# A gated MLP in two passes over its width, its factors fetched one by one, its instructions in a fixed order

## The chip, the cores and the metric

The kernel runs on one core of a Trainium2 chip. Its time is device microseconds of one execution; the median of three runs of the kernel before is 918.9 us (915.48 to 921.77).

## The reference

Attention, a first MLP and a second, gated MLP follow one another on 2304 tokens of width 512; the second MLP is what the change rewrites.

```python
x = attention(q, k, v, M_prev, z_prev, beta)          # 4 x 576 tokens, 8 heads of 64
h = x @ w_in                                          # 512 -> 1024
e = exp(h - max(h)); solu = h * e / sum(e)
x = layernorm(solu) * g_ln @ w_out                    # 1024 -> 512
gate = 1 / (1 + exp(-(x @ w_gate)))                   # 512 -> 1536
out = (gate * (x @ w_val)) @ w_out2                   # 1536 -> 512
```

The weights of both MLPs arrive as 64-bit floats; the chip has none, so the kernel builds 32-bit values out of their integer halves.

## The kernel before, in words

**Precision.** Products run in a reduced 32-bit format. Each operand is split into a high part (a cast, on ACT) and a low part (value minus high part, on DVE or GpSimd), and a product is three matmuls: high x high, high x low, low x high.

**Attention** (to about 200 us) and the **first MLP** (to about 451 us) come first. The first MLP goes through 18 blocks of 128 tokens: hidden products (line 634), statistics on DVE, ACT and GpSimd, transposes (681), the output product (691, copied out at 697). Its steps are a list; the conversions of the first six width blocks of the second MLP (`EARLY = 6`) are merged evenly into it from step 60 on.

**The second MLP** cuts its width 1536 into 12 blocks of 128 (`f`) and the tokens into three groups of 768 (`s`), each in halves of 384. One unit is one (`s`, `f`). Value and gate of a unit are 2 x 2 block products over (halves of tokens, halves of width 512), done with seven products instead of eight: `left` names the weight sides v1, g0, g1, s1 to s4, sums of the blocks, and b11, t1, ... the token sides. Each product is six matmuls of 384 columns (893) into one of two PSUM buffers. ACT copies the first out (910), DVE's additions the others (912, 914, 916, 919, 920, 931, 938), ACT applies the sigmoid (936), GpSimd multiplies gate and value (942), `hilo` splits the result G (138 on ACT, 139 on DVE). `project` (951) multiplies G by the output factor into six PSUM banks, one for 128 tokens, which gather all 12 units of a group; these 18 matmuls are slipped between the products of the next unit by `fill`. So 36 units stand in three segments of 12.

**Conversion** of a block `f` (`convert`, `stage`): three raw loads (104: value, gate, output), for each two DVE operations (108, 109), two on ACT (112, 792), two on DVE (117, 122) and a multiplication on GpSimd (794); four GpSimd sums (808 to 811); a cast of all seven sides on ACT (815) and one GpSimd subtraction over 1792 columns for their low parts (816); the same for the output block (821, 822). The result stands in a ring of buffers (`ring_g`, `ring_o`) and is stored to DRAM (832), from where later segments fetch it (837), seven sides in one DMA of 1792 KB. Blocks 6 to 11 are converted in the first segment, while its units run; `prep` hands out their steps at each `fill`.

**Between segments** `xsplit` builds the next group's token sides: differences on GpSimd (859), casts on ACT (852), low parts on DVE (853).

**Order.** All DMAs are issued by SP's queue. Attention's instructions stand in a written order (`manual_schedule`); those of both MLPs are ordered by the framework's planner by its own costs. Each engine takes its instructions strictly in the order of its queue.

Of the kernel before, what the change touches and what calls it, by code (L numbers as in the profile page):

```python
# [32 lines left out]
def f32(ap):  # L33
    return ap.bitcast(F32)
# [13 lines left out]
def kernel(  # L48
# [16 lines left out]
    nc = tc.nc  # L65
# [36 lines left out]
    def load_raw(raw, src):  # L102
        a = src.shape[1]
        nc.sync.dma_start(raw.rearrange("p (a n) t -> p a (n t)", a=a), src)
# [478 lines left out]
    class Moe1:  # L583
# [33 lines left out]
        def hidden(self, t):  # L617
# [21 lines left out]
            def stats():  # L639
# [13 lines left out]
                sq = sb.tile([P, F1], BF16, tag="sq", name=f"sq{t}", bufs=1)  # L653
# [10 lines left out]
        def lntrans(self, t):  # L664
# [3 lines left out]
            def half(h):  # L668
                if t % GB == 0 and h == 0:

                    if g == 2:
                        L = [self.spare.tile([P, NF1, GW], F32R, tag="gv", name=f"lnT{g}{x}", bufs=2) for x in range(2)]
# [74 lines left out]
    EARLY = 6  # L747

    class Moe2:

        def __init__(self, ra, w3, xe, scr):
            self.ra, self.w3, self.xe, self.scr = ra, w3, xe, scr
            self.n, self.rb = [0, 0], None
            self.W, self.x, self.G = {}, None, {}
            self.tt, self.ttag = xe, "xs"
            self.dram = {}

        def ring_g(self, f):
            k = self.n[0]
            self.n[0] += 1  # L760
            pool = self.ra if self.rb is None else (self.ra, self.ra, self.rb)[k % 3]
            t = pool.tile([P, 2, 7, 2 * P], F32R, tag="gv", name=f"gv{f}_{k}", bufs=2 if pool is self.ra else 1)
            self.W.setdefault(f, [None, None])[0] = t
            return t

        def ring_o(self, f):
            k = self.n[1]
            self.n[1] += 1
            pool = self.ra if self.rb is None else (self.ra, self.w3, self.w3)[k % 3]
            t = pool.tile([P, 2, DM], F32R, tag="w3", name=f"wo2{f}_{k}", bufs=1 if pool is self.ra else 2)  # L770
            self.W.setdefault(f, [None, None])[1] = t
            return t

        def scratch(self, f):
            if f not in self.dram:
                self.dram[f] = [
                    self.scr.tile([P, 2, w], F32, tag=f"{x}{f}", name=f"scr{x}{f}") for x, w in (("g", 14 * P), ("o", DM))
                ]
            return self.dram[f]

        def convert(self, f, cv):

            st = {}

            def stage(src, dst):
                raw = cv.tile([P, 512, 2], I32, tag="raw", name="raw2", bufs=2)
                ex = cv.tile([P, 2, 512], I32, tag="ex", name="ex2", bufs=2)
                e, m = ex[:, 0], ex[:, 1]
                load_raw(raw, src)
                f64_a(raw, e, m)  # L790
                f64_r(e)
                nc.scalar.mul(f32(m), m, 2.0**-20)  # L792
                f64_b(raw, e, m, 2.0**-20)
                nc.gpsimd.tensor_mul(f32(m) if dst is None else dst, f32(m), f32(e))  # L794
                return f32(m)

            def val():
                st["gv"] = self.ring_g(f)
                st["M"] = cv.tile([P, 8, 2 * P], F32, tag="M", name=f"M{f}")
                src = moe2_w_val[:, 2 * f * P : 2 * (f + 1) * P].rearrange("(c p) f -> p c f", p=P)  # L800
                stage(src, st["M"][:, 0:2].rearrange("p a n -> p (a n)"))

            def gate():
                src = moe2_w_gate[:, 2 * f * P : 2 * (f + 1) * P].rearrange("(c p) f -> p c f", p=P)
                M = st["M"]
                stage(src, M[:, 2:4].rearrange("p a n -> p (a n)"))
                v0, v1, g0, g1, s1, s2, s3, s4 = (M[:, i] for i in range(8))
                nc.gpsimd.tensor_add(s1, v0, v1)
                nc.gpsimd.tensor_sub(s3, g0, v0)
                nc.gpsimd.tensor_sub(s2, s1, g0)  # L810
                nc.gpsimd.tensor_sub(s4, g1, s2)

            def split():
                gv, M = st["gv"], st["M"]
                nc.scalar.copy(gv[:, 0], M[:, 1:8])  # L815
                nc.gpsimd.tensor_sub(gv[:, 1], M[:, 1:8], f32(gv[:, 0]))  # L816

            def outp():
                o = self.ring_o(f)
                m = stage(moe2_w_out[f * P : (f + 1) * P, :].unsqueeze(1), None)  # L820
                nc.scalar.copy(o[:, 0], m)
                nc.gpsimd.tensor_sub(o[:, 1], m, f32(o[:, 0]))

            return [val, gate, split, lambda: self.save(f, 0)], [outp, lambda: self.save(f, 1)]

        def both(self, f, x):
            t = f32(self.W[f][x])
            return (t if x else t.rearrange("p x b n -> p x (b n)")), self.scratch(f)[x]

        def save(self, f, x):  # L830
            t, d = self.both(f, x)
            nc.sync.dma_start(d, t)

        def fetch(self, f, x):
            (self.ring_o if x else self.ring_g)(f)
            t, d = self.both(f, x)
            nc.sync.dma_start(t, d)

        def xsplit(self, s, xp):

            n0, nh = s * SG // 64, HT // 64
            self.nx = nx = {}

            def src(k, h):
                return X[:, n0 + h * nh : n0 + (h + 1) * nh, 2 * k : 2 * k + 2].rearrange("p n c t -> p c n t")

            def shape(t):
                return t.rearrange("p c (n t) -> p c n t", t=64)

            def parts(nm, x):  # L850
                hi, lo = (shape(t) for t in self.pair(nm, s, xp))
                nc.scalar.copy(hi, x)
                nc.vector.tensor_sub(lo, x, f32(hi))

            tt = {}

            def diff(nm, a, b):
                t = tt[nm] = shape(self.tt.tile([P, 2, HT], F32, tag=self.ttag, name=f"T{nm}{s}"))
                nc.gpsimd.tensor_sub(t, a, b)

            b11, b12, b21, b22 = src(0, 0), src(0, 1), src(1, 0), src(1, 1)

            def one():
                diff("t1", b12, b11)
                parts("b11", b11)
                diff("t2", b22, tt["t1"])

            def two():
                parts("t2", tt["t2"])
                parts("t1", tt["t1"])  # L870
                diff("t4", b21, tt["t2"])

            def three():
                parts("b21", b21)
                diff("t3", b22, b12)
                parts("t3", tt["t3"])

            def four():
                parts("b22", b22)
                parts("t4", tt["t4"])  # L880

            return [one, two, three, four]

        def pair(self, nm, s, xp):
            t = [xp.tile([P, 2, HT], F32R, tag="xx", name=f"x{nm}{x}{s}") for x in "hl"]
            self.nx[nm] = t
            return t

        def product(self, nm, W, blk, xb):
            po = self.ps.tile([P, 512], F32, tag="h", name=nm)[:, :HT]  # L890
            for c in range(2):
                for n, (w, x) in enumerate(((0, 0), (0, 1), (1, 0))):
                    nc.tensor.matmul(  # L893
                        po, W[:, w, blk, c * P : c * P + P], xb[x][:, c],
                        start=c + n == 0, stop=c == 1 and n == 2,
                    )
            return po

        def unit(self, s, f, fill, last=False):
            W, x = self.W[f][0], self.x  # L900
            sg = self.xe.tile([P, 2, HT], F32, tag="e", name=f"sg{s}_{f}")
            vl = self.xe.tile([P, 2, HT], F32, tag="xs", name=f"vl{s}_{f}")
            p1, u, u3, u5 = (self.tm.tile([P, HT], F32, tag=t, name=f"{t}{s}_{f}") for t in ("p1", "u", "u3", "u5"))
            left = dict(zip(("v1", "g0", "g1", "s1", "s2", "s3", "s4"), range(7)))

            def prod(w, b):
                return self.product(f"{w}_{s}_{f}", W, left[w], x[b])
# [21 lines left out]
            if last:  # L929
                nc.scalar.activation(sg[:, 0], sg[:, 0], AF.Sigmoid)  # L930
# [161 lines left out]
```

## Time and profile before

| | |
|---|---|
| median of three runs | 918.9 us |
| profiled execution | 917.98 us, its span 915.8 us, mean granted clock 0.983 |
| busy: PE, DVE, ACT, POOL | 855.6, 622.7, 471.8, 443.2 us |
| bytes moved by DMA | 134.13 MB, mean 146 GB/s |

The span is what the profile shows of the execution; 2.2 us of the execution's time lie around it. PE is TensorE, POOL GpSimd. A granted clock of 1.00 is TensorE's full 2.4 GHz.

### The profile page before, as it was taken

How to read it: one execution, taken by the hardware profiler on the slowest of the kernel's cores; microseconds unless marked ns; L12 is line 12 of the kernel's file. 1: busy time of each engine (PE TensorE's matmuls, PEld its weight loads, DVE VectorE, ACT ScalarE, POOL GpSimd, SP SyncE). 2: the span in 40 equal slices, each digit the busy share in tenths (PEclk: the TensorE clock that was granted, in tenths of full speed). 3: DMA queues.
4: the chain of work that ended last, by engine and by line, in shares of the span. 5: the costliest groups of instructions: out<-in, count | busy, mean ns of one | idle time of the engine just before them, and what ended most of it. 6: DMA issues, size and time to landing. Idle time of an engine off the chain costs nothing.

```text
span 915.8 us, 14684 instructions
## 1 busy us (share of the span) xinstructions
PE 855.6 (93%) x5308; PEld 739.4 (81%) x5308; DVE 622.7 (68%) x1332; ACT 471.8 (52%) x972; POOL 443.2 (48%) x451
## 2 busy tenths in 40 slices
PE   6999999998899999998977887899999999999996
PEld 5777777766689988788867676787999998999995
DVE  7899999978976479975378868748444447444443
ACT  6899999985775567757333432433111124111112
POOL 5677787772625078786077655783111111111110
PEclk8999999999999999999999999999999999999999
DMA  6444444412203036552257657350755550655531
GB/s 142 108 94 109 105 106 107 102 36 92 91 26 116 24 127 230 198 194 104 69 178 275 247 196 275 127 207 22 254 207 208 211 202 25 236 206 211 204 117 69
DMA packets 93384, 134.13 MB, mean 146 GB/s; under 512 B 63872, under 2 KB 76416, under 8 KB 88704
## 3 DMA queue, kind: packets, MB, share of 16 engines
q1 hardware_dynamic: 93312, 133.20, 44.0%
q8 instruction: 42, 0.69, 0.3%
q14 instruction: 30, 0.25, 0.1%
HBM read 100.15 MB, written 33.03 MB: 145 GB/s over the span
## 4 chain that ended last, share of the span: by engine, by line
PE 69%; DVE 15%; issue 6%; ACT 4%; POOL 3%; DMA 2%; SPq 0%; DVEq 0%; POOLq 0%; ACTq 0%
PE acc L951 14%; PE s L893 13%; PE g L893 6%; PE po L691 6%; PE h L634 6%; PE x L486 5%; PE sc L377 4%; PE v L893 3%; PE x L471 2%; DVE ex L108 2%; DVE ex L117 2%; DVE ex L122 2%; DVE ex L109 2%; DMA raw<-in_moe_w_val_dram 1%; PE sc L368 1%
## 5 line engine op out<-in xcount | busy, mean ns | idle before, releaser
L942 POOL TENSOR_TENSOR vl<-vl,sg 128x768 f32<-128x768 f32 x35 | 66.9, 1912 | 239.3 <-DVE vl L938 229.6
L951 PE MATMUL acc<-wo,G 128*128 128x512 f32 x648 | 160.2, 393 | 2.9 <-ACT G L138 2.4
L951 PEld LDWEIGHTS acc<-wo,G 128*128 128x128 f32 x648 | 121.7, 190 | 25.4 <-ACT G L138 3.3
L936 ACT ACTIVATE sg<-sg 128x768 f32<-128x768 f32 x35 | 29.6, 847 | 193.0 <-DVE sg L931 193.0
L416 POOL TENSOR_SCALAR p<-p,rs,o 128x256 f32<-128x256 f32 (+2 forms) x144 | 91.7, 652 | 5.9 <-DVE rs L411 1.8
L634 PE MATMUL h<-wih,xs 128*128 128x512 f32 x288 | 84.3, 404 | 4.5 <-DVE e L651 4.5
L406 ACT ACTIVATE p<-p,nm 128x128 f32<-128x128 f32 (+2 forms) x144 | 82.8, 584 | 0.4 <-DVE nm L399 0.4
L691 PE MATMUL po<-lnT,woh 128*128 128x256 f32 x432 | 79.4, 283 | 0.0
L919 DVE TENSOR_TENSOR vl<-s,u 128x384 f32<-128x384 f32 x36 | 20.0, 555 | 71.1 <-PE s L893 71.1
L634 PEld LDWEIGHTS h<-wih,xs 128*128 128x128 f32 x288 | 53.8, 191 | 17.6 <-DVE e L651 3.6
L691 PEld LDWEIGHTS po<-lnT,woh 128*128 128x128 f32 x432 | 67.4, 192 | 0.2
L112 ACT ACTIVATE ex<-ex,ebias 128x512 int32<-128x512 int32 (+1 forms) x56 | 36.3, 648 | 52.9 <-DVE ex L108 52.8
L691 PE MATMUL po<-lnT,wol 128*128 128x256 f32 x216 | 61.2, 283 | 0.0
L816 POOL TENSOR_TENSOR gv<-M,gv 128x1792 fp32r<-128x1792 f32 x12 | 51.1, 4256 | 15.7 <-ACT gv L815 15.7
L893 PE MATMUL g<-xb21h,gv 128*128 128x384 f32 x144 | 44.4, 349 | 13.4 <-DVE u L912 13.4
L399 DVE CUSTOM_DVE_ANT_0 p<-sc,mask 128x128 f32<-128x128 f32 (+3 forms) x128 | 54.6, 480 | 1.5 <-PE sc L377 1.5
L117 DVE SCALAR_TENSOR_TENSOR ex<-raw,ex 128x512 int32<-128x512 int32 (+1 forms) x56 | 47.8, 853 | 6.8 <-ACT ex L112 6.6
L794 POOL TENSOR_TENSOR M<-ex 128x512 f32<-128x512 f32 x24 | 31.8, 1328 | 38.7 <-PE s L893 22.3
L893 PE MATMUL s<-xt2h,gv 128*128 128x384 f32 x144 | 43.9, 346 | 6.5 <-DVE vl L938 6.3
L122 DVE SCALAR_TENSOR_TENSOR ex<-raw,ex 128x512 f32<-128x512 uint16 (+1 forms) x56 | 49.3, 880 | 0.6 <-ACT ex L792 0.4
L912 DVE TENSOR_TENSOR u<-s,p 128x384 f32<-128x384 f32 x36 | 20.0, 555 | 42.4 <-PE s L893 40.5
L893 PE MATMUL v<-xt4h,gv 128*128 128x384 f32 x144 | 43.9, 346 | 4.8 <-DVE u L920 4.8
(385 smaller groups left out, 2361.6 us busy)
## 6 DMA issues: line engine op xcount, KB each, us to landing
gv<-scrg SPq DMA_DIRECT2D x24, 1792.0 KB, 7.3
scrg<-gv SPq DMA_DIRECT2D x12, 1792.0 KB, 6.6
wo<-scro SPq DMA_DIRECT2D x25, 512.0 KB, 3.4
raw<-in_moe_w_val_dram SPq DMA_DIRECT2D x12, 512.0 KB, 4.5
raw<-in_moe_w_gate_dram SPq DMA_DIRECT2D x12, 512.0 KB, 3.8
raw<-in_moe_w_out_dram SPq DMA_DIRECT2D x12, 512.0 KB, 3.8
scro<-wo SPq DMA_DIRECT2D x12, 512.0 KB, 6.4
out_dram<-X SPq DMA_DIRECT2D x18, 256.0 KB, 2.6
```

Of the source, the lines that this page charges most:

```text
L117: nc.vector.scalar_tensor_tensor(ex, top, -0x80000000, ex, ALU.bitwise_and, ALU.bitwise_or)
L122: nc.vector.scalar_tensor_tensor(f32(mt), low, 2.0**-16 * scale, f32(mt), ALU.mult, ALU.add)
L399: nc.vector.tensor_tensor_reduce(p, x, m, -1.0, 3.0e38, ALU.add, ALU.min, nm)
L406: nc.scalar.activation(p, p, AF.Exp, bias=nm, scale=-1.0, accum_out=self.sum[n % 2][:, c, 0:1])
L416: nc.gpsimd.tensor_scalar(p, p, r["rs"][:, c : c + 1], og, ALU.mult, ALU.mult)
L486: nc.tensor.matmul(r["x", g][64 * hh : 64 * hh + 64, c0 : c0 + src.shape[1]], r["vt"][:, c : c + D], src, start=False, stop=j == 0,)
L634: nc.tensor.matmul(ph[:, j * 512 : j * 512 + 512], xs[:, s, c], w[:, j * 512 : j * 512 + 512], start=(c == 0 and s == 0 and w is hi), stop ...
L691: nc.tensor.matmul(po, w[:, m * P : m * P + P], L[x][c // 4][:, c % 4], start=(c == 0 and n == 0), stop=(c == NF1 - 1 and n == 2),)
L816: nc.gpsimd.tensor_sub(gv[:, 1], M[:, 1:8], f32(gv[:, 0]))
L893: nc.tensor.matmul(po, W[:, w, blk, c * P : c * P + P], xb[x][:, c], start=c + n == 0, stop=c == 1 and n == 2,)
L942: nc.gpsimd.tensor_mul(vl, vl, sg)
L951: nc.tensor.matmul(po, G[:, x, sl], o[:, w], start=k + n == 0, stop=k == NFC - 1 and n == 2)
```

## The change

The second MLP runs in two passes over its width. Blocks 0 to 6 are computed for token groups 0, 1 and 2; in group 2 blocks 7 to 11 follow at once; then groups 1 and 0 get blocks 7 to 11. That makes five segments of 7, 7, 12, 5 and 5 units. Groups 0 and 1 leave the first pass with partial sums, which are stored to DRAM and loaded back into X in the second unit of their second segment; the last output is an addition on DVE. The last two blocks of a segment are the first two of the next, in reverse, and stay in the ring.

Factors always go through DRAM. A ring holds 17 single weight sides (256 KB each); after each product a further load is issued when the 17th product before has been emitted. Blocks 0 to 5 are converted in the first MLP (from step 50 on, ending 14 steps sooner), one step after another; blocks 6 to 11 in units 1 to 19, their steps at set places (`hook`) of the units, their loads and stores issued by ACT. GpSimd's conversion work is cut into pieces of 256 columns, the gating into two of 384, the token differences likewise. The token sides of the next segment are built at the hooks of a segment's last unit, the differences in the four units before. The gate's low parts come after the next unit's first products (`late`). The whole second MLP is traced under `manual_schedule`: its order is the program's.

Of the diff, the removed lines (the bodies of `Moe2` above) are left out:

```diff
...
+    NA = 7
+    USE = ("g0", "s2", "s1", "g1", "s3", "s4", "v1")
...
+    NRING = 17
...
+                def three():
...
+                    for h in range(2):
+                        sl = slice(256 * h, 256 * h + 256)
+                        nc.gpsimd.tensor_mul(out[:, sl], m[:, sl], e[:, sl])
...
+            def split(hi, src):
+                nc.scalar.copy(hi, src)
+                for a in range(0, src.shape[1], 256):
+                    sl = slice(a, a + 256)
+                    nc.gpsimd.tensor_sub(src[:, sl].bitcast(F32R), src[:, sl], f32(hi[:, sl]))
...
+            def put(a, b):
+                def go():
+                    if a == 1:
+                        st["hi"] = cv.tile([P, 7, 2 * P], F32R, tag="hi", name=f"hi{f}")
+                    split(flat(st["hi"], a - 1, b - 1), flat(st["M"], a, b))
+                    if b == 8:
+                        dma.dma_start(d[0][:, :, 0], f32(st["hi"]))
+                        self.owed = [lambda: dma.dma_start(d[0][:, :, 1], st["M"][:, 1:]), lambda: self.saved.add((f, 0))]
...
+            return loads, [
+                v[0], v[1], lambda: (new_m(), v[2]()), g[0], g[1], lambda: (g[2](), sums(0)), o[0],
+                lambda: sums(1, 2), lambda: (o[1](), sums(3)), put(1, 3), o[2], put(3, 5), put(5, 7), put(7, 8), put_o,
+            ]
...
+        def fetch(self):
+            while self.nl < len(self.loads) and (self.nl < NRING or self.loads[self.nl - NRING][2] == 0):
+                ld = self.loads[self.nl]
+                f, w = ld[:2]
+                if (f, 0) not in self.saved:
+                    return
+                ld[3] = self.ring.tile([P, 2, 2 * P], F32R, tag="gv", name=f"gv{f}{w}_{self.nl}", bufs=NRING)
+                nc.sync.dma_start(f32(ld[3]), self.dram[f][0][:, BLK[w]])
+                self.nl += 1
...
+            nc.scalar.copy(p1, self.product(n, f, "g0"))
+            self.late[0]()
+            hook(0)
+            add(u, self.product(n, f, "s2"), p1)
+            self.late[1]()
+            fill(), hook(1)
+            add(u5, self.product(n, f, "s1"), u)
+            fill(), hook(2)
+            add(sg[:, 0], self.product(n, f, "g1"), p1)
+            nc.scalar.activation(sg[:, 0], sg[:, 0], sig)
+            fill(), hook(3)
+            po = self.product(n, f, "s3")
             add(vl[:, 1], po, u5)
             add(u3, po, u)
+            fill(), hook(4)
+            add(sg[:, 1], self.product(n, f, "s4"), u5)
+            nc.scalar.activation(sg[:, 1], sg[:, 1], sig)
+            nc.gpsimd.tensor_mul(vl[:, 1], vl[:, 1], sg[:, 1])
+            fill(), hook(5)
+            add(vl[:, 0], self.product(n, f, "v1"), u3)
+            nc.gpsimd.tensor_mul(vl[:, 0], vl[:, 0], sg[:, 0])
+            hi(1)
+            fill(), hook(6)
+            self.late = (lambda: (hi(0), lo(1))), (lambda: lo(0))
...
+            slots = [(i, j) for i in range(1, 3 * NA - 1) if i not in ends for j in (0, 1, 2, 3, 5, 6)]
...
+            n0, n1 = 50, len(steps) - 2 * NC - 2
...
+            n2 = n1 - 14
+            first, conv = m2.conversion(range(EARLY), cv)
+            merge(steps[n0:n2], m1.queue([lambda: [x() for x in first], *conv]))
...
+    first, conv = m2.conversion(range(EARLY, NFC), cv, nc.scalar)
+    m2.start()
+    for x in first:
+        x()
+    with tc.manual_schedule():
+        m2.run(xp, tp, conv)
```

## Rows read from the trace of the kernel before

**Rows 1.** The page: busy us, share of the span, instructions of each engine.
```profile
PE 855.6 (93%) x5308; PEld 739.4 (81%) x5308; DVE 622.7 (68%) x1332; ACT 471.8 (52%) x972; POOL 443.2 (48%) x451
```

**Rows 2.** Windows: stretch, length, busy of PE, PEld, DVE, ACT, POOL; clock, DMA share, GB/s.
```profile
451.85:641.52 189.67, 159.25 (x764) 139.25 (x763) 141.43 (x185) 69.61 (x97) 120.39 (x75) 0.96 0.53 191
641.52:893.84 252.32, 251.63 (x1322) 234.71 (x1321) 108.44 (x185) 53.84 (x76) 40.73 (x23) 1.00 0.53 188
```

**Rows 3.** Source view of line 910: min/median/max ns, first and last start.
```profile
L910 ACT COPY p<-g x36: 455/480/482, 451.8 to 893.8; 128x384 f32<-128x384 f32 x36
```

**Rows 4.** Timeline of ACT, 638 to 655 us: start, length, instruction.
```profile
641.52 0.48 ACT L910 COPY p<-g 128x384 f32<-128x384 f32 x1 [1.48 <-PE g L893]
652.90 0.48 ACT L910 COPY p<-g 128x384 f32<-128x384 f32 x1 [0.69 <-PE g L893]
```

**Rows 5.** Waits of PE, 452 to 640 us: total us, times, longest.
```profile
PE g L893 <- DVE u L912: 12.9, 8, 3.4
PE s L893 <- DVE vl L938: 6.3, 4, 3.6
```

**Rows 6.** Timelines of DVE and of POOL, 540 to 552 us.
```profile
544.98 4.54 DVE L122 SCALAR_TENSOR_TENSOR ex<-raw,ex 128x512 f32<-128x512 uint16 x1
544.46 4.51 POOL L816 TENSOR_TENSOR gv<-M,gv 128x1792 fp32r<-128x1792 f32 x1
```

**Rows 7.** Source views from 340 us on: conversion and low parts on DVE.
```profile
L108 DVE TENSOR_SCALAR ex<-raw x29: 412/502/3821, 345.4 to 587.2; 128x512 int32<-128x512 int32 x29
L117 DVE SCALAR_TENSOR_TENSOR ex<-raw,ex x29: 676/745/3467, 348.6 to 589.9; 128x512 int32<-128x512 int32 x29
L122 DVE SCALAR_TENSOR_TENSOR ex<-raw,ex x29: 671/683/4543, 349.2 to 590.5; 128x512 f32<-128x512 uint16 x29
L139 DVE TENSOR_TENSOR G<-vl,G x37: 553/948/3948, 472.3 to 906.1; 128x768 fp32r<-128x768 f32 x35, 128x384 fp32r<-128x384 f32 x2
```

**Rows 8.** Groups by form, 452 to 915 us: busy us, mean ns.
```profile
L912 DVE TENSOR_TENSOR u<-s,p 128x384 f32<-128x384 f32 x36 | 20.0, 555 | 42.4 <-PE s L893 40.5 <-ACT p L910 1.9
L112 ACT ACTIVATE ex<-ex,ebias 128x512 int32<-128x512 int32 x18 | 13.0, 722 | 41.9 <-DVE ex L108 41.9
L853 DVE TENSOR_TENSOR xb21l<-X,xb21h 128x768 fp32r<-128x768 f32 x2 | 1.9, 947 | 0.0
```

**Rows 9.** Source views of three POOL lines.
```profile
L816 POOL TENSOR_TENSOR gv<-M,gv x12: 4015/4068/4822, 323.0 to 595.3; 128x1792 fp32r<-128x1792 f32 x12
L809 POOL TENSOR_TENSOR M<-M x12: 732/806/1457, 280.6 to 588.4; 128x256 f32<-128x256 f32 x12
L942 POOL TENSOR_TENSOR vl<-vl,sg x35: 1840/1849/2548, 465.0 to 893.4; 128x768 f32<-128x768 f32 x35
```

**Rows 10.** Chain of waits: start, length, work; units around the second change.
```profile
743.85 2.08 PE s L893 x12
...
791.11 2.08 PE s L893 x12
```

**Rows 11.** The page, part 6: DMA issues, KB each, median us to landing.
```profile
gv<-scrg SPq DMA_DIRECT2D x24, 1792.0 KB, 7.3
scrg<-gv SPq DMA_DIRECT2D x12, 1792.0 KB, 6.6
wo<-scro SPq DMA_DIRECT2D x25, 512.0 KB, 3.4
out_dram<-X SPq DMA_DIRECT2D x18, 256.0 KB, 2.6
```

**Rows 12.** Timeline of SP, 638 to 645 us, and windows around it.
```profile
638.97 3.08 SPq L956 DMA_DIRECT2D out_dram<-X  x6
639.00:643.00 4.00, 4.00 (x24) 3.96 (x23) 2.12 (x4) 1.52 (x4) 1.85 (x1) 1.00 0.82 305
642.00:650.00 8.00, 8.00 (x42) 7.29 (x41) 3.47 (x6) 0.84 (x2) 0.98 (x1) 1.00 0.89 322
```

**Rows 13.** Windows: the second half of the first MLP.
```profile
335.00:451.00 116.00, 109.89 (x777) 102.06 (x777) 86.07 (x115) 73.87 (x123) 78.84 (x72) 1.00 0.43 157
```

More of the change, by code (lines that the diff above doesn't have):

```diff
@@ L747 @@
     EARLY = 6
-    class Moe2:
[L751 to L763, printed above, removed]
-            return t
[L766 to L890, printed above, removed]
@@ L891, in product @@
             for c in range(2):
[L892 removed]
+                for i, (a, b) in enumerate(((0, 0), (0, 1), (1, 0))):
                     nc.tensor.matmul(
[L894 to L918 removed]
@@ new lines, in run @@
+        def run(self, xp, tp, conv):
+            segs, work = self.segs, []
+            nothing = lambda: None
+            self.late = (nothing, nothing)
+            units = [(n, s, k, f) for n, (s, fs) in enumerate(segs) for k, f in enumerate(fs)]
+            tbs = (3, 4, 5, 0, 1, 2)
+            ends = [sum(self.len[: n + 1]) - 1 for n in range(len(segs))]
+            slots = [(i, j) for i in range(1, 3 * NA - 1) if i not in ends for j in (0, 1, 2, 3, 5, 6)]
+            when, m = {}, 0
+            per = len(conv) // (NFC - EARLY)
+            n0 = per
+            for j, step in enumerate(conv):
+                at = j * n0 // per if j < per else n0 + (j - per) * (len(slots) - n0) // (len(conv) - per)
+                when.setdefault(slots[at], []).append(step)
@@ new lines, in run, with hook @@
+            carry = []
+            os = self.os
+            for i, (n, s, k, f) in enumerate(units):
+                if k == 0:
+                    self.x, self.nx = self.nx, {}
+                left = self.len[n] - 1 - k
+                more = n + 1 < len(segs)
+                pre = {}
+                if more and left == 4:
+                    d = self.diffs(segs[n + 1][0], tp)
+                if more and 0 < left < 5:
+                    pre[0] = [d[4 - left]]
+                if carry:
+                    pre.setdefault(0, []).append(carry.pop())
+                if more and left == 0:
+                    pre = {j: [x] for j, x in enumerate(self.parts(segs[n + 1][0], xp))}
+                    carry.append(pre.pop(7)[0])
+                if n >= NSG and k == 1:
+                    pre.setdefault(6, []).append(lambda s=s: self.partials(s))
+                def hook(j):
+                    for step in pre.get(j, []) + when.get((i, j), []):
+                        step()
+                final = i == len(units) - 1
+                G = self.unit(n, f, nothing if final else fill, hook)
+                while work:
+                    work.pop(0)()
+                o = os.pop()
+                work += [lambda n=n, s=s, k=k, G=G, o=o, tb=tb: self.project(n, s, k, G, o, tb) for tb in tbs]
+                if not final:
+                    os.append(self.fetch_o(units[i + 1][3], i + 1))
@@ L1007, in staged @@
+            for x in self.late:
+                x()
+            for w in work:
+                w()
     def staged(pool, nm):
```

299 lines of the change are left out of this document (194 added, 105 removed).

## The prediction

> **What bounds the kernel now.** I read the page first: over the whole span TensorE is busy 93% [rows 1], so the question is where it is not. The windows view splits the second MLP at its 14th unit [rows 2]: from 641.52 us on TensorE is busy 251.63 of 252.32 us, before that 159.25 of 189.67 us. The beat of the units is read from ACT's copy of the first product (line 910): 36 copies, the first at 451.8, the last at 893.8 us [rows 3], the 14th at 641.52 and the next 11.38 us later [rows 4]. So 22 late intervals take 252.3 us, 11.38 us each but for one change of token group, and that is TensorE without a gap: the floor of a unit. The 13 early intervals take 189.7 us, 14.6 each. **The excess is 189.7 - 13 x 11.38 = 41.8 us**, and it lies where factors 6 to 11 are converted.
>
> What makes it: TensorE's longest waits there are for DVE's additions that empty PSUM [rows 5]. An addition itself always takes 0.555 us [rows 8], so it is late, not slow. It stands in DVE's queue behind conversion work, and that is stretched: at 544.98 us a line-122 operation took 4.54 us beside a GpSimd split that ran from 544.46 for 4.51 us [rows 6]; its median is 0.683 and its longest 4.543, and lines 117, 108 and the low part of G (139) reach 3.5 to 3.9 us in the same way [rows 7]. DVE and GpSimd exclude each other, and what DVE loses at once is as long as the GpSimd instruction.
>
> **Part 1: conversion thinner and in small pieces.** Before, six conversions lie in 13 intervals. Now factor 6 is spread over 15 places in units 1 to 3 (2.5 units), the other five over the remaining places up to unit 19 (about 2.9 units each), none in a unit that ends a pass. DVE per unit: seven additions of 0.555 and the low part of G 0.948 make 4.83 us [rows 7, 8]; a conversion adds at most 3 x (2 x 0.502 + 0.745 + 0.683) = 7.3 us [rows 7], so 7.3/2.9 = 2.5, or 2.9 for factor 6: 7.3 to 7.8 us of 11.38. GpSimd: 19 pieces at 0.806 plus the gating 1.849 [rows 9], so 15.3/2.9 + 1.85 = 7.1 us. That leaves the mutual exclusion. Six DVE operations a unit read twice from SBUF (two low parts, four of the conversion). At worst each waits for a whole piece: 6 x 0.81 = 4.8, sum 12.3, over the floor. On average a piece is running 63% of the time and half is left: 6 x 0.63 x 0.4 = 1.5, sum about 9. The second is nearer to the medians of rows 7, which are hardly above the minima.
>
> Does TensorE still wait? A product takes 2.08/2 = 1.04 us [rows 10]; one product with its filler takes 11.38/7 = 1.63. Its PSUM buffer is wanted two products on, 2 x 1.63 - 1.04 = 2.2 us after its end; the addition takes 0.555, so DVE may be late by 1.65 us. A step of the kind `two` is 0.745 + 0.683 + at worst one piece 0.81 = 2.24 us, 0.6 too much; there are three in a conversion, so 6 x 3 x 0.6 = 11 us at worst, 0 at best. I take 5. So **-41.8 + 5 us**.
>
> **Part 2: two passes, five segments.** 36 units stay 36, but the four changes of tokens stand where two did. Four intervals with a change took 791.11 - 743.85 = 47.26 us, 1.74 more than four plain ones [rows 10]. In the last unit of a segment DVE carries seven low parts of X at 0.95 [rows 8] beside its 4.8: 11.5 us, as much as the floor; with a lock on each (7 x 0.8) up to 5.6 us spills. Two more changes cost 0 to 19 us (four at 5.6 less two at 1.74); I take the price of the one seen: **+3.5 us**. The 12 partial sums go out and come back as 24 transfers of 256 KB on SP, which issues one in about half a microsecond [rows 12]; the loads stand a unit ahead of their use, so no wait. If they came late, the additions at the end of segment 3 would hold the PSUM banks of segment 4. The 12 additions replace copies of the same width: 0 but at the end.
>
> **Part 3: factors through the ring.** Seven loads of 256 KB a unit instead of one of 1792 KB: SP's issue time rises from 2 to 8 issues, some 4 us of 11.38; behind a waiting load on SP stand only later loads, output factors, partial sums and results, none due within a unit. A load waits for the 17th product before it, 17 x 1.63 = 28 us ahead; one of 1792 KB lands in 7.3 us and one of 256 KB in 2.6 [rows 11]. The first two units no longer find their factors in SBUF: the first load may wait for buffers of the first MLP, 0 (they come free while its last projection runs) to 6.0 us (3.4 + 2.6, [rows 11]); I take **+1**. The loads and stores of the late conversions move to ACT's queue, seven a conversion. No row shows a DMA issued by ACT; bounded by 0 and SP's half microsecond, it is at most 3.5/2.9 = 1.2 us a unit on an engine busy 69.61 of 189.67 us [rows 2]. A store there can wait for GpSimd's last piece, 0.8 us, and holds up ACT's copy and sigmoids; within the slack, 0. ACT's conversion instructions are as before (0.72 for the first, [rows 8]).
>
> **Part 4: first MLP and the end.** The early conversions start ten steps sooner and stop 14 sooner, with one M and one high buffer that are held until their stores land (6.6 us, [rows 11]). TensorE idles 116 - 109.9 = 6.1 us there [rows 13], so at most 6 can be won; at most 6 x 6.6 = 40 us of GpSimd could be lost, of which I let a quarter reach TensorE: -6 to +10, taken 0. At the end GpSimd gates one half (0.92 instead of 0.555) and DVE adds all six blocks: **+1** (0 to 2).
>
> **Sum**, against the profiled execution's own 917.98 us (0.9 below the median of 918.9): 917.98 - 41.8 + 5 + 3.5 + 1 + 1 = 886.7, so 887 us. With every extra at nothing and the first MLP at its best it is 870; with two of the upper bounds met about 903.
>
> **Rivals.** *(a) The excess goes with the number of conversions, not with how closely they stand.* There are six as before, 41.8/6 = 7 us each; in a fixed order no engine steps past a late instruction. For it: DVE waits for ACT and GpSimd inside each conversion whatever the spacing. Against: the splits of 4.07 us [rows 9] are gone, and the medians of rows 7 are short. If half stays: 917.98 - 20.9 + 3.5 + 2 = 903. If all stays: 923.
>
> *(b) The DMA engines become the bound: slower.* Units 0 to 19 need 16 factor sets of 1.84 MB, 20 output factors of 0.52, six raw sets of 1.57, six stored sets of 2.36 and 3.1 MB of partial sums: 66.6 MB in 20 x 11.4 = 228 us, 292 GB/s, where the early stretch now moves 191 [rows 2]. Place: TensorE waits for the ring in segments 0 and 1. It decides below 66.6/(228 + 41) = 248 GB/s, where the whole gain is gone; at 240 it takes 277 us, 49 more: 936. For it: a 1792 KB load alone gives 1.835 MB/7.3 us = 251 GB/s. Against: six transfers of 256 KB were issued in 3.08 us [rows 12] and landed in a median of 2.6 us [rows 11], so they overlap, and the stretches around them moved 305 and 322 GB/s at a share of 0.82 and 0.89 [rows 12]; and the ring holds 4.5 MB in hand. The Trainium skill speaks for this rival: DMA: Bandwidth & Descriptors (section Bandwidth) advises batches of 1 MiB or more, and SBUF — State Buffer (The DMA setup-cost knee) gives 224 GB/s at 256 KiB; at that rate, an estimate, the 66.6 MB take 297 us and the sum would be 956. The overlapping transfers of rows 12 don't agree with that rate as a ceiling.
>
> *(c) The first MLP pays more than I let it*: its small GpSimd statistics queue behind a piece that waits for a store; 897 to 910.
>
> **Chances.** My forecast 0.62 (870 to 903); (a) half 0.12, (a) all 0.08; (b) 0.10; (c) 0.05; below 870, by a first MLP that gains more than its visible idle time, 0.03. A measurement of this kernel tells about 1% (9 us) from no change. Faster: 0.62 + 0.12 + 0.03 + most of (c) = 0.80; within 1%: (a) all and the rest of (c), 0.10; slower: (b), 0.10. The range that holds 8 in 10 runs from 869, every extra at nothing, to 910, which takes in (a) half and (c).
>
> **What would show it.** Right: line-910 copies about 11.4 to 11.8 us apart from the first to the last unit, with some 2 us more at four places; no DVE operation of the conversion above about 1.6 us; the windows of the second MLP with TensorE over 97% busy at full granted clock. Part 2 is wrong if units 6, 13, 25 or 30 take over 14 us; part 3 if TensorE or SP waits stand on the ring's loads, with a DMA share near 1; part 4 if the first copy of line 910 is not within 6 us before or 10 us after 451.8. The forecast fails if the early units stay above 13 us, whatever waits then stand ahead of the products.

## The result, and the profile after

The changed kernel takes 886.05 us (median of four runs, 884.14 to 890.37) against 920.34 (915.48 to 921.93) of the kernel before in the same session: ratio 0.9643 [0.959, 0.9695], faster. The profiled execution took 885.51 us, its span is 883.7. The forecast was 887. The total was right; of the three pieces below none was, and their errors cancel. One of the four runs of a kernel below (whole in after) took 1178.99 us at a mean granted clock of 0.654 and is left out of its row. From here on "first copy" and "last copy" are the first and last of ACT's 36 copies of a unit's first product (line 910 before, 967 after). They cut the span into three pieces:

| us | before | after | difference | forecast |
|---|---|---|---|---|
| start to first copy | 451.85 | 446.35 | -5.5 | 0 |
| the 35 intervals | 441.90 | 418.99 | -22.9 | -41.8 + 5 + 3.5 + 1 = -32.3 |
| last copy to end | 22.05 | 18.36 | -3.7 | +1 |
| span | 915.8 | 883.7 | -32.1 | -31.3 |

The busy line of the page, the source view of the copy, and the windows (length, then PE, PEld, DVE, ACT, POOL; clock, DMA share, GB/s) of the second MLP up to its 19th unit, from there on, and of the end of the first MLP, all of after; they answer to [rows 1], [rows 3], [rows 2] and [rows 13]:

```profile
PE 848.7 (96%) x5308; PEld 738.2 (84%) x5308; DVE 631.5 (71%) x1391; ACT 497.3 (56%) x1092; POOL 503.6 (57%) x636
...
L967 ACT COPY p<-g x36: 459/482/483, 446.4 to 865.3; 128x384 f32<-128x384 f32 x36
...
446.35:671.39 225.04, 209.92 (x1064) 190.33 (x1063) 155.08 (x249) 91.76 (x170) 136.80 (x149) 0.98 0.79 271
671.39:865.34 193.95, 193.95 (x1022) 181.61 (x1021) 114.59 (x181) 57.42 (x109) 69.40 (x68) 1.00 0.59 201
335.00:446.35 111.35, 110.20 (x784) 103.07 (x783) 62.09 (x94) 65.42 (x119) 64.64 (x93) 1.00 0.37 125
```

The last 17 intervals are 193.95 us of TensorE without a gap, 11.4 each, and two of the changes of segment lie among them. The first 18, in which factors 6 to 11 are converted, take 225.0 us where a floor of 7.9 for the first (no projection goes with it) and 11.4 for each other would be 201.7: 23.3 over. By the same reckoning, at its own floor of 11.38, the 13 early intervals of before were 45.2 over. So the conversions cost 7.5 us each before and 3.9 now, not the 5 us in all of the forecast. Of the 23.3, TensorE is idle for 15.1; in the other 8.2 the same matmuls take longer.

What stretches them shows at 486 to 495 us. Timelines of ACT with its DMA issues, of DVE and of PE, then windows, of after (in brackets the idle time ahead of an instruction and what ended it):

```profile
486.04 0.52 ACTq L830 DMA_DIRECT2D scrg<-M  x1
486.60 0.62 ACT L815 CAST ho<-ex 128x512 fp32r<-128x512 f32 x1 [5.38 <-POOL M L818]
...
488.83 0.34 ACTq L839 DMA_DIRECT2D scro<-ex  x1
489.22 0.72 ACT L112 ACTIVATE ex<-ex,ebias 128x512 int32<-128x512 int32 x1 [1.05 <-POOL ex L818]
...
489.98 0.69 DVE L117 SCALAR_TENSOR_TENSOR ex<-raw,ex 128x512 int32<-128x512 int32 x1 [3.09 <-ACT ex L112]
490.58 0.69 DVE L122 SCALAR_TENSOR_TENSOR ex<-raw,ex 128x512 f32<-128x512 uint16 x1
491.19 0.55 DVE L986 TENSOR_TENSOR vl<-v,u 128x384 f32<-128x384 f32 x1
...
491.79 0.44 PE L946 MATMUL s<-xt2h,gv4s 128*128 128x384 f32 x1 [2.05 <-DVE vl L986]
...
488.00:492.00 4.00, 1.95 (x11) 1.51 (x10) 1.76 (x3) 1.82 (x4) 1.84 (x3) 1.00 0.90 305
493.00:495.00 2.00, 2.00 (x7) 1.71 (x6) 2.00 (x3) 1.18 (x3) 2.00 (x4) 0.50 0.81 255
```

Read it from the top. ACT's next instruction is a DMA, the store of M's low part, which waits for GpSimd's last piece of the split (818); ACT computes nothing for 5.38 us (1.1 of it are the issues of two stores, 0.59 and 0.52), and for another 1.05 at the last store (839), which waits for GpSimd too. So line 112 is late, DVE waits 3.09 us for it with line 117 at the head of its queue, the addition 986 behind that has a finished product in PSUM but can't run, and TensorE stands 2.05 us for the buffer. Then comes the second price: after a stretch in which TensorE was busy for 1.95 of 4 us, the granted clock is 0.50, its level of 1.2 GHz, and seven matmuls fill two microseconds. Windows of after show two such stretches, 492.7 to 496.1 and 660.0 to 663.4 us; 6.8 us at half clock lose some 3.4 of the 8.2. What makes the rest was not taken apart.

The locks are gone. Source views of the conversion on DVE and of GpSimd's pieces, of after, from 446 us on (min/median/max ns); they answer to [rows 7] and [rows 9]:

```profile
L117 DVE SCALAR_TENSOR_TENSOR ex<-raw,ex x18: 675/692/1498, 456.7 to 675.1; 128x512 int32<-128x512 int32 x18
L122 DVE SCALAR_TENSOR_TENSOR ex<-raw,ex x18: 676/685/1512, 457.3 to 675.8; 128x512 f32<-128x512 uint16 x18
L818 POOL TENSOR_TENSOR M<-M,hi x42: 731/742/1117, 474.7 to 687.5; 128x256 fp32r<-128x256 f32 x42
```

The longest line 122 is 1.51 us, not 4.54: as forecast. What remains is waits. TensorE's own in that stretch (446 to 660 us, of after: total us, times, longest), which answer to [rows 5]:

```profile
PE acc L999 <- DVE G L965: 6.6, 6, 1.9
PE s L946 <- DVE vl L986: 3.4, 2, 2.0
PE s L946 <- ACT p L967: 2.8, 3, 1.2
```

The additions are no longer the longest; the projection's wait for DVE's low part of G is. None of TensorE's waits in this stretch is for a DMA.

### The profile page after: what moved, and what is told of

It is laid out like the page before. It is cut to its first block, busy times and chain, and to the rows that moved or that the text cites. A ratio compares the mean times of both kernels' runs of the same rounds, so it can differ in the third digit from the quotient of the medians.

```text
span 883.7 us, 15617 instructions
## 1 busy us (share of the span) xinstructions
PE 848.7 (96%) x5308; PEld 738.2 (84%) x5308; DVE 631.5 (71%) x1391; ACT 497.3 (56%) x1092; POOL 503.6 (57%) x636
## 4 chain that ended last, share of the span: by engine, by line
PE 66%; POOL 12%; DVE 9%; DMA 7%; issue 3%; ACT 2%; ACTq 0%; SPq 0%; DVEq 0%; POOLq 0%
PE s L946 12%; PE acc L999 12%; PE po L691 7%; PE h L634 6%; PE g L946 6%; PE x L486 5%; PE sc L377 4%; POOL M L818 3%; PE v L946 3%; PE x L471 2%; POOL Tt L887 2%; DMA part<-ev 2%; POOL M L812 1%; PE sc L368 1%; POOL M L798 1%
## 5 line engine op out<-in xcount | busy, mean ns | idle before, releaser
L999 PE MATMUL acc<-o,G 128*128 128x512 f32 x648 | 183.8, 393 | 6.6 <-DVE G L965 6.6
L984 POOL TENSOR_TENSOR vl<-vl,sg 128x384 f32<-128x384 f32 x36 | 38.2, 1060 | 214.0 <-ACT sg L983 213.9
L999 PEld LDWEIGHTS acc<-o,G 128*128 128x128 f32 x648 | 119.6, 189 | 19.4 <-DVE G L965 9.3
L976 ACT ACTIVATE sg<-sg 128x384 f32<-128x384 f32 x36 | 18.9, 525 | 105.2 <-DVE sg L975 100.8
L965 DVE TENSOR_TENSOR G<-vl,G 128x384 fp32r<-128x384 f32 x72 | 60.1, 835 | 18.3 <-ACT G L962 18.2
L818 POOL TENSOR_TENSOR M<-M,hi 128x256 fp32r<-128x256 f32 x84 | 66.1, 811 | 2.2 <-ACT hi L815 2.0
L983 ACT ACTIVATE sg<-sg 128x384 f32<-128x384 f32 x36 | 18.9, 526 | 77.8 <-DVE sg L982 77.8
L962 ACT CAST G<-vl 128x384 fp32r<-128x384 f32 x72 | 37.1, 515 | 43.0 <-POOL vl L984 36.9
L798 POOL TENSOR_TENSOR M<-ex 128x256 f32<-128x256 f32 x48 | 39.3, 838 | 34.1 <-DVE ex L122 15.2
L634 PE MATMUL h<-wil,xs 128*128 128x512 f32 x144 | 45.8, 399 | 0.0
L325 POOL TENSOR_TENSOR G<-E,zm 128x640 f32<-128x640 f32 x16 | 24.8, 1552 | 35.4 <-DVE E L322 30.6
```

What stands on the lines that cost most here:

```text
L634: nc.tensor.matmul(ph[:, j * 512 : j * 512 + 512], xs[:, s, c], w[:, j * 512 : j * 512 + 512], start=(c == 0 and s == 0 and w is hi), stop ...
L798: nc.gpsimd.tensor_mul(out[:, sl], m[:, sl], e[:, sl])
L818: nc.gpsimd.tensor_sub(src[:, sl].bitcast(F32R), src[:, sl], f32(hi[:, sl]))
L965: nc.vector.tensor_sub(G[:, 1, hs[h]], vl[:, h], f32(G[:, 0, hs[h]]))
L999: nc.tensor.matmul(po, G[:, x, sl], o[:, w], start=first and i == 0, stop=stop and i == 2)
```

## The experiments

Each was compared with the kernel before on the same chip, where that took a median of 916.93 to 920.34 us, so the ratio compares two kernels better than their times do. The third column is the time from the first to the last copy in the one profiled execution, the fourth what it is over that of the kernel without late conversions (395.5). Runs of one kernel lie up to 7 us apart; a difference of 2 or 3 us between two kernels is not shown by one profile each.

| kernel | us (range) | 35 intervals | over | ratio to before |
|---|---|---|---|---|
| before | 920.34 | 441.90 | 46.4 | 1 |
| after | 886.05 (884.14 to 890.37) | 418.99 | 23.5 | 0.9643 [0.959, 0.9695] |
| pieces in before | 910.07 (909.32 to 910.48) | 431.0 | 35.5 | 0.9924 [0.9909, 0.9939] |
| whole in after | 894.22 (893.25 to 895.4) | 428.45 | 32.9 | 0.9753 [0.9735, 0.9771] |
| no late conversion | 862.33 (860.4 to 862.8) | 395.54 | 0 | 0.94 [0.9381, 0.942] |
| one pass | 928.0 (925.52 to 928.63) | 460.88 | 65.3 | 1.0109 [1.0091, 1.0126] |
| dense | 916.91 (915.89 to 922.06) | 450.68 | 55.1 | 0.9997 [0.9981, 1.0014] |
| wide | 893.6 (893.26 to 894.72) | 427.31 | 31.8 | 0.9741 [0.9726, 0.9755] |
| planner's order | 911.1 (910.13 to 913.04) | 441.19 | 45.7 | 0.9932 [0.9915, 0.9949] |
| stores on SP | 880.74 (880.24 to 881.77) | 415.61 | 20.1 | 0.9607 [0.9592, 0.9621] |
| stores on SP, wide | 875.67 (874.6 to 877.01) | 408.1 | 12.6 | 0.9546 [0.9517, 0.9574] |
| stores on SP, two M | 876.01 (874.73 to 877.38) | 408.75 | 13.2 | 0.9545 [0.9519, 0.9571] |
| first MLP merged as before | 893.71 (892.52 to 899.38) | 417.88 | 22.3 | 0.975 [0.9711, 0.9789] |
| stores on SP, wide, two M | 873.01 (871.26 to 874.5) | 406.45 | 10.9 | 0.9493 [0.9475, 0.951] |

The theory was my prediction's: GpSimd's long instructions lock DVE (A), and the conversions stand too closely (density, B). The rival: the in-order queues make a conversion's own chain of waits reach TensorE (C).

### Pieces alone, before and after

In before, GpSimd's conversion is cut; in after, it is made whole again:

```diff
# pieces in before
-                nc.gpsimd.tensor_sub(gv[:, 1], M[:, 1:8], f32(gv[:, 0]))
+                for i in range(7):
+                    nc.gpsimd.tensor_sub(gv[:, 1, i], M[:, 1 + i], f32(gv[:, 0, i]))
...
# whole in after
-                    for h in range(2):
-                        sl = slice(256 * h, 256 * h + 256)
-                        nc.gpsimd.tensor_mul(out[:, sl], m[:, sl], e[:, sl])
+                    nc.gpsimd.tensor_mul(out, m, e)
...
```

> The kernel before with one part alone: GpSimd's conversion work (multiplications of 512 columns, the split of 1792, the output split of 512) in pieces of 256 columns; order, two DMAs, one pass as before. Theory A (the long GpSimd instruction that locks DVE out makes most of the 41.8 us of early excess): 895 to 905 us, no conversion operation on DVE over 2 us. Theory B (density and the planner's order make it; the lock only moves the wait): 912 to 925 us, although the long DVE operations are gone.

> The kernel after with GpSimd's conversion work whole again: multiplications of 512 columns, one split of 1792 at the last step, output split of 512; all else as after. Theory A: 896 to 905 us, DVE operations of 3 to 4.5 us are back, and the first MLP ends some 5 us later (451 instead of 446). Theory B: 884 to 891 us.

Line 122 in the first, and line 108, the longest of the conversion, and the copy in the second (source views):

```profile
L122 DVE SCALAR_TENSOR_TENSOR ex<-raw,ex x29: 675/1045/1240, 348.9 to 583.3; 128x512 f32<-128x512 uint16 x29
```

```profile
L108 DVE TENSOR_SCALAR ex<-raw x18: 413/662/2908, 453.4 to 679.3; 128x512 int32<-128x512 int32 x18
L966 ACT COPY p<-g x36: 457/480/483, 444.6 to 873.1; 128x384 f32<-128x384 f32 x36
```

Pieces are worth 10.9 us of intervals in before and 9.5 in after: about a quarter of the excess. The first came out between the two expectations (lines 117 and 108 still reach 2.3 and 2.0 us), the second just below the range of theory A. Theory A's sign is there in the second: the low part of G (line 964) takes 3.1, 3.1 and 3.8 us in three places, where the longest of after is 1.4. The locks were real and the smaller part. In before the first copy came 2.6 us later with pieces; in after, whole, it came 1.7 us earlier, not the 5 later that theory A had; the 1.7 show nothing, since kernels with the same first MLP lie between 444.3 and 446.4. Whether pieces cost the first MLP a little was not followed up.

### No late conversion

```diff
-                for f in range(NFC)
+                for f in range(EARLY)
...
+            for f in range(EARLY, NFC):
+                self.dram[f] = self.dram[f - EARLY]
...
-    first, conv = m2.conversion(range(EARLY, NFC), cv, nc.scalar)
+    first, conv = [], []
...
```

> The kernel after without the conversion of blocks 6 to 11 (they use the stored factors of blocks 0 to 5, so that part of the result is another); units, DMAs of the ring and segments are as after. If the early intervals are long because of the conversions (three us each): 864 to 870 us, 11.4 us from unit 3 on. If the changes of segment and the ring's loads make them long: 878 us or more, with intervals of 12 us and more left among the first 18.

The copy and a window of it:

```profile
L969 ACT COPY p<-g x36: 464/480/482, 446.1 to 841.7; 128x384 f32<-128x384 f32 x36
...
446.11:659.00 212.89, 212.82 (x1123) 199.49 (x1122) 117.90 (x190) 60.85 (x115) 58.13 (x54) 1.00 0.59 193
```

TensorE has no wait at all, at full clock. The whole excess of after hangs on the six conversions (their DMA traffic, some 24 MB, is gone here with their instructions; this run doesn't part the two). The intervals on both sides of a change of segment are 11.30 to 11.46 us: without conversions beside them, changes cost nothing, where I had +3.5. Better than expected.

### Room and order: one pass, dense, wide, planner

One pass is the change without its two passes, three segments of 12; dense and wide only move the hooks of factors 6 to 11 together or apart; the planner's order drops the written one.

```diff
# one pass
-            A, B = list(range(NA)), list(range(NA, NFC))
+            A, B = [0, 1, 2, 3, 4, 6, 5, 7, 8, 9, 10, 11], []
...
# dense: range(1, 13); wide: range(1, 23)
-            slots = [(i, j) for i in range(1, 3 * NA - 1) if i not in ends for j in (0, 1, 2, 3, 5, 6)]
+            slots = [(i, j) for i in range(1, 13) if i not in ends for j in (0, 1, 2, 3, 5, 6)]
...
# planner's order
-    with tc.manual_schedule():
-        m2.run(xp, tp, conv)
+    m2.run(xp, tp, conv)
```

> The kernel after in one pass: three segments of 12 units, no partial sums; blocks in the order 0 1 2 3 4 6 5 7 8 9 10 11, so the six late conversions must stand in units 1 to 10, 1.7 units each; pieces, ring, fixed order, queues as after. Density theory (a conversion costs the more the closer it stands to the next; without any the units run at 11.4): the early excess grows from 23 to 35 us or more, 898 to 912 us. Count theory (some 4 us for each conversion wherever it stands): 884 to 890 us, like after.

> The kernel after with its late conversions packed into units 1 to 12 instead of 1 to 19: 2.5 units for the first, 1.7 for each of the others; two passes as they are. Density theory: 895 to 908 us. Count theory: 884 to 890 us.

> The kernel after with its late conversions spread over units 1 to 22: 2.5 units for the first, 3.4 for each of the others. Density theory: 878 to 883 us. Count theory: 885 to 888 us.

> The kernel after with the planner ordering the second MLP instead of the written order (manual_schedule taken away); program otherwise the same. If the written order is part of the gain (the planner lets conversion steps bunch up ahead of additions): 892 to 910 us. If the spacing in the program text does it all: 883 to 889 us. If the written order is what makes engines wait (ACT's stores): below 882 us.

Waits of PE in one pass and in dense (total us, times, longest):

```profile
PE g L946 <- DMA gv11g<-scrg: 10.7, 1, 10.7
```

```profile
PE v L946 <- DVE u L980: 14.5, 3, 8.3
...
PE s L946 <- DVE u L973: 11.7, 3, 5.5
```

With the passes kept and the same pieces and order, conversions put into units 1 to 12 cost 9.2 us each (55.1/6) and into units 1 to 19 they cost 3.9: the whole gain of the change is gone in dense. One pass, with units 1 to 10 for them, is worse than before, partly because factor 11 comes too late for its first use (10.7 us). So the passes work by the room they give. But both came out above what density gave them. In dense ACT stands 22.3 us in five waits for GpSimd's split ahead of M's store (waits of ACT ahead of line 815; in after 6.1 us in two), so a part of its price may be theirs. And wide, which should have gained by it, lost 7.5 us. One interval of wide, 24.14 us long, shows why. Timelines of ACT and PE, a window, and the DMA issues of that stretch (KB, us to landing), of wide:

```profile
645.70 0.35 ACTq L838 DMA_DIRECT2D scro<-ho  x1
646.09 0.52 ACT L983 ACTIVATE sg<-sg 128x384 f32<-128x384 f32 x1 [9.07 <-DMA scrg<-hi]
...
648.28 1.65 PE L999 MATMUL acc<-o,G 128*128 128x512 f32 x3 [7.36 <-ACT G L962]
...
630.00:646.00 16.00, 10.92 (x58) 10.01 (x57) 4.87 (x10) 2.49 (x5) 6.43 (x9) 1.00 1.03 356
...
scrg<-hi ACTq DMA_DIRECT2D x1, 896.0 KB, 13.0
```

The store of the high part landed after 13.0 us, in a stretch in which the ring's and the other transfers held the DMA engines at a share of 1.03. The output block's store (838) went out as it landed, at 645.6 us; in the trace both carry the same semaphore. The sigmoid behind that store stood 9.07 us. So a DMA on ACT can hold ACT for the landing of another DMA, not only for its own data.

The planner's order, with the passes, the pieces and the spacing all in, is nearly as far over as before (45.7), a little above its first range: the written order is worth 25 us. Of the 22.2 us that its intervals are longer than after's, 8.4 lie in the last 17 (202.3 us against 193.95), where no conversion runs. Its last copy is at 887.50 and its span 908.3, so its end is 20.8 us, 2.4 longer than after's 18.36.

### Stores off ACT

```diff
-                        dma.dma_start(d[0][:, :, 0], f32(st["hi"]))
+                        nc.sync.dma_start(d[0][:, :, 0], f32(st["hi"]))
... # the four stores of a late conversion; its raw loads stay on ACT
```

> The kernel after with the late conversions' four stores on SP's queue; their raw loads stay on ACT's. Theory C (a store issued by ACT waits for GpSimd's last piece, so ACT's next conversion instruction, then DVE's and then an addition that empties PSUM come late): 877 to 883 us, and no ACT instruction of line 112 waits for GpSimd's line 818. Rival (the store's wait now holds SP and the ring's loads come late; or ACT's wait was covered anyway): 885 to 892 us.

> The kernel after with the late stores on SP's queue and the late conversions spread over units 1 to 22. If the wider spacing failed only because ACT's queue stood behind stores that landed late (one interval of 24 us), the density theory holds after all: 873 to 879 us, no interval above 16 us. If wider spacing hurts by itself (conversion work meeting the loads after the second change of segment): 884 to 893 us.

The copies of the two:

```profile
L967 ACT COPY p<-g x36: 457/480/482, 444.7 to 860.3; 128x384 f32<-128x384 f32 x36
```

```profile
L967 ACT COPY p<-g x36: 460/482/483, 446.3 to 854.4; 128x384 f32<-128x384 f32 x36
```

At the change's own spacing this is 5 us by the times, 3.4 by the intervals and 3.3 by the ratios, whose 95% ranges overlap; no line-112 instruction waits for line 818 any more, as expected. At the wide spacing it is 18 us, and wide now beats narrow as density wants. Theory C holds for the stores, and A and B hold beside it: what was refuted is either alone.

### Two buffers for M

With stores on SP, POOL's first multiplication of a conversion still waited for the store of M before it. Wait of POOL in that kernel (in after it is 10.7 us in two):

```profile
POOL M L798 <- DMA scrg<-M: 9.5, 2, 5.8
```

```diff
-    NRING = 17
+    NRING = 14
...
-                st["M"] = cv.tile([P, 8, 2 * P], F32, tag="M", name=f"M{f}")
+                st["M"] = cv.tile([P, 8, 2 * P], F32, tag="M", name=f"M{f}", bufs=1 if dma is nc.sync else 2)
```

> The kernel after with the late stores on SP and two M buffers for the late conversions (their room comes from the ring: 14 sides instead of 17). If GpSimd's wait for M's store (9.5 us in two waits with the stores on SP) is what holds DVE and TensorE: 873 to 878 us. If it is covered, or the shorter ring costs as much: 879 to 884 us.

That wait is gone and the intervals lost 6.9 us, as expected; three ring buffers fewer cost nothing that shows.

### The first MLP's merge

```diff
-            n0, n1 = 50, len(steps) - 2 * NC - 2
+            n0, n1 = 60, len(steps) - 2 * NC - 2
...
-            n2 = n1 - 14
+            n2 = n1
```

> The kernel after with the early conversions merged into the first MLP as before: from step 60 to the same last step (n0 = 60, n2 = n1). If these two numbers make the first MLP end 5.5 us sooner: the first copy of line 967 at 450 us or later and 889 to 893 us. If the finer steps or the freed buffers make it: the first copy at 444 to 448 us and 884 to 888 us.

The copy of it, and the same window of the first MLP in it, in before and in after:

```profile
L967 ACT COPY p<-g x36: 458/482/483, 454.5 to 872.3; 128x384 f32<-128x384 f32 x36
...
380.00:420.00 40.00, 34.85 (x231) 31.59 (x230) 29.80 (x46) 26.85 (x48) 32.90 (x47) 0.97 0.46 152
```

```profile
380.00:420.00 40.00, 37.75 (x247) 33.94 (x246) 32.37 (x49) 25.69 (x43) 30.07 (x27) 1.00 0.49 178
```

```profile
380.00:420.00 40.00, 39.82 (x279) 36.87 (x278) 28.24 (x42) 27.13 (x48) 30.41 (x41) 1.00 0.31 102
```

The first copy is 8.1 us later with the old merge points, the intervals stay. So the 5.5 us won in the first MLP are two points of a list: starting ten steps sooner and stopping 14 sooner brings 8.1, and the rest of the change takes 2.6 of it back there. Pieces alone cost 2.6 in before too; that the cause is the same is not shown.

### The best version

Stores on SP, the wide spacing and two M buffers together, the edits as above.

> Stores on SP, late conversions over units 1 to 22, two M buffers with a ring of 14 sides, all three at once. If the two gains (875.7 and 876.0 from 880.7) lie on different waits they add: 870 to 873 us. If both take away the same one (GpSimd's wait for M's store, which wider spacing also gives time to): 874 to 877 us.

The copy, and its largest wait of PE up to 700 us:

```profile
L967 ACT COPY p<-g x36: 461/483/484, 446.4 to 852.8; 128x384 f32<-128x384 f32 x36
...
PE acc L999 <- DVE G L965: 2.8, 2, 2.1
```

873.01 us: 0.9493 [0.9475, 0.951] of before, better than both kernels. It lies between the ranges of the two theories: the two cures overlap in part (two M take 6.9 us off the intervals at the narrow spacing, 1.7 at the wide). Read the other way, with the stores on SP the wide spacing is worth 7.5 us of intervals with one M and 2.3 with two, so most of that went through the wait for M.

## Why the prediction was right, and where it was not

**The sum** was right within 1 us only because its errors cancel: the intervals gave 9.4 us less than forecast (-22.9 for -32.3), the first MLP and the end 10.2 more (-9.2 for +1). That is luck, and the signs that the prediction named for the second MLP were not there: eight of the first 18 intervals are over 13 us (up to 15.1) where nearly all were to be 11.4 to 11.8, and TensorE is busy 93% of them (209.92 of 225.04 us) at a mean clock of 0.98, not over 97% at full clock.

**The floor.** I took 11.38 us for all 13 early intervals. The first has no projection and is 7.9 us in after, so the excess was 45.2, not 41.8.

**Part 1: the step that failed is "does TensorE still wait? ... I take 5".** It counted DVE's load and one piece of GpSimd, and 23.3 us stayed. What it left out are DMAs that compute engines wait for. The chain at 486 us crosses three in-order queues: a store on ACT waits for GpSimd's piece, the conversion step on ACT behind the store is late, DVE stands with it at the head of its queue, the addition that frees PSUM stands behind. By the runs, one after the other, taking the stores off ACT is worth 3.4 us of the 23.5 in the table, a second buffer for M, whose store GpSimd waits for, another 6.9, and the wider spacing 2.3 more; 10.9 remain, and their cause is open but for the partial sums below. Pieces alone were worth 9.5 to 10.9. I had also left out what a gap brings after it: matmuls at a granted clock of 0.50, some 3.4 us. That the locks would go was right, and that the room matters was right (dense).

**Part 2.** +3.5 was 0 for what it priced: no unit before a change stands out, and the kernel without late conversions passes its changes in 11.30 to 11.46. Which part of my 11.5 us of DVE work in such a unit was covered was not tried. But the unit after the first change takes 15.12 us, the longest of all, and there the partial sums, which I put at nothing, do count. Their copies out of PSUM (line 1006) go through two buffers, and DVE waits for the stores of the copies before. Its waits in the second MLP, and TensorE's at 545 us, of after:

```profile
DVE ev L1006 <- DMA part<-ev: 6.2, 4, 2.1
...
545.03 0.50 PE L999 MATMUL acc<-o,G 128*128 128x512 f32 x1 [1.91 <-DVE G L965]
```

Ahead of the wait at 545 us DVE stood 2.10 and 1.24 us for such stores, then ran two conversion steps and the low part of G. Three waits of TensorE come after such copies (0.88 at 540, 1.91 at 545 and 1.32 at 634 us): 4.1 of its 15.1 us, of which the conversion steps between have their part. In the best version the largest one is still there, 2.08 us. Without late conversions DVE does not wait there; more than two buffers were not tried.

**Part 3.** "A store there ... within the slack, 0" was wrong: 3.4 us of the intervals at the change's spacing, 19.2 at the wide one. The wait I priced at a piece, 0.8 us, was over 4 us at 486 us (5.38 less the two issues). "+1" for the first loads was 0: the first interval is 7.89 us, and no wait of TensorE stands on the ring. What stands at the second unit is ACT's queue again, this time behind a raw load:

```profile
467.23 0.38 ACTq L104 DMA_DIRECT2D raw<-in_moe_w_val_dram  x1
467.70 0.48 ACT L967 COPY p<-g 128x384 f32<-128x384 f32 x1 [2.50 <-DMA gv3s<-scrg]
468.24 0.45 PE L946 MATMUL s<-xt1h,gv2s 128*128 128x384 f32 x1 [1.08 <-ACT p L967]
...
454.00:467.70 13.70, 13.16 (x69) 11.83 (x67) 10.13 (x19) 5.18 (x10) 6.68 (x8) 1.00 1.01 376
```

(timelines of ACT and of PE, and the window ahead of them, of after.) The raw load went out as a load of the ring, with which it shares a semaphore in the trace, landed at 467.15 us; the copy behind it came 2.50 us late, and TensorE stood 1.08. Every variant of the changed kernel that converts late has its raw loads on ACT; elsewhere they were not tried. The ring held.

**Part 4.** The bound of -6 for the first MLP was the right end of the range, and 0 the wrong choice. The end was -3.7, not +1. Timelines of PE and DVE at the end, of before and of after:

```profile
905.66 4.36 PE L951 MATMUL acc<-wo,G 128*128 128x512 f32 x18 [1.66 <-ACT G L138]
909.15 1.89 DVE L955 COPY X<-acc 128x512 f32<-128x512 f32 x3 [2.48 <-PE acc L951]
```

```profile
871.68 8.32 PE L999 MATMUL acc<-o,G 128*128 128x512 f32 x36
876.64 4.09 DVE L1012 TENSOR_TENSOR X<-acc,X 128x512 f32<-128x512 f32 x6 [1.75 <-PE acc L999]
```

Before, TensorE waits 1.66 us for the last G and then projects 18 times; after, the 18 projections of the unit before stand in front, 36 without a gap while G is made, and the additions start at the first finished block. The planner's order with the same code ends 2.4 us later, so most of the 3.7 is the written order; the rest was not tried.

**The rivals.** *(a) half* met its premise, half of the excess stayed, and its 903 was missed by the terms of parts 2 to 4. Its reason, a price for each conversion whatever the spacing, fell with dense against the change: the same six conversions cost 9.2 and 3.9 us each. Its other sentence, that in a fixed order no engine steps past a late instruction, is what the trace shows. *(b)* fell: the first 18 units moved 271 GB/s at a DMA share of 0.79, over the 248 at which it decides, and no wait of TensorE there is for the ring; the window above reached 376 GB/s at a share of 1.01. By the Trainium skill, SBUF — State Buffer (The DMA setup-cost knee), transfers of 256 KiB give 224 GB/s; this window, most of whose transfers are of 256 KB and some of 512, does not agree with that as a ceiling for many at once. But the DMA engines are no longer far off: in the wide kernel's 24 us interval they stood at a share of 1.03 when a store landed late. *(c)* went the other way.

**Open:** how much of dense's 55 us is ACT's stores (it was not run with them on SP); what the last 10.9 us of the best version are, of which its PE waits on DVE's low part of G (2.8, with 2.08 of it behind the partial sums) are the largest entry; what the raw loads on ACT cost; and how the 25 us of the written order divide among its parts.

## What to carry to other kernels

A DMA that must wait, for its own data or for another DMA, belongs on a queue with no compute behind it, above all when the work behind it feeds another engine's queue: here its price was 3.4 us at one spacing and 19.2 at another. Side work costs by the room between its steps and by the order they stand in: pieces alone gave back about a quarter of the excess, and without the room that the passes give, or without the written order, all or most of the change's gain was gone. When a sum comes out right, check its terms by cutting the span at the same events before and after; here all three were off.

## What the runs showed of the hardware that I had not expected

- After TensorE had been busy for 1.95 of 4.00 us, the granted clock was 0.50 from 493 to 495 us, though TensorE was then busy throughout.
- A stretch of 13.7 us, in which 4.62 of 5.16 MB went through SP's queue, mostly as loads of 256 KB, moved 376 GB/s at a DMA share of 1.01.
- Three DMAs on ACT's queue went out within 0.1 us of the landing of an earlier DMA that has the same semaphore in the trace: raw loads at 460.34 and 467.23 us of after, behind ring loads of SP's queue that landed at 460.24 and 467.15, and wide's store at 645.70, behind one of ACT's that landed at 645.62.
- A store of 896 KB landed in a median of 6.2 us from ACT's queue, and in 13.0 us where the DMA share was 1.03:

```profile
scrg<-hi ACTq DMA_DIRECT2D x6, 896.0 KB, 6.2
scrg<-M ACTq DMA_DIRECT2D x6, 896.0 KB, 7.5
```

(the page of after, DMA issues.)
